# mLSTM and squared-ReLU FFN on one core: DRAM copies cut into 5 KB pieces and moved later, weights' fetches ahead of the loads of squares and of x's store

## The chip, the cores and the metric

The kernel runs on one core of a Trainium2 chip. The metric is the device time of an execution in microseconds (us); lower is better. The profile is one further execution with every instruction and DMA recorded; its span is 1 to 2 us below the device time.

## The reference, cut to what matters

```python
# 4 batches x 8 heads x 768 tokens x 40; k, q, v, gates, o_gate in float32
for t in range(S):                       # mLSTM: a recurrence per head
    C = f_stab * C + i_stab * outer(v_t, k_t);  n = f_stab * n + i_stab * k_t
    y_t = sigmoid(o_t) * (C @ q_t) / max(|n . q_t|, 1)
x = y.transpose(0, 2, 1, 3).reshape(3072, 320)
return (relu(x @ w_in) ** 2) @ w_out     # 320 -> 2048 -> 320; float64 weights
```

## The kernel before

The 3072 rows are 24 steps of 128 tokens. The mLSTM of a step gives x (128 x 320). The FFN works on groups of two steps: a first-layer product `ffn1` (reads x transposed, `xT`) and a second-layer product `ffn2` or `ffn2_fast` (makes the output y). Steps 0 to 5 form a start in which the weights are also brought in and rounded piece by piece (ScalarE, VectorE, GpSimd). From step 6 on, a loop runs four parts for each step `s` (`at` is 0 to 3): even steps carry an `ffn1`, odd steps a second layer. In this loop nothing is transposed on TensorE: k, q and x go through DRAM, come back as 32 x 32 squares side by side, and VectorE turns the squares.

```python
def pair_up(s):                          # a copy inside DRAM: heads in pairs
    b, c = divmod(s, NB)
    for n, src in enumerate((k, q)):
        nc.sync.dma_start(
            kq_d[s, n].rearrange("two j t d -> two j (t d)"),
            src[b, :, c * P : (c + 1) * P, :].rearrange("(j two) t d -> two j (t d)", two=2))

def squares_in(s, n, dst):               # four loads of squares from kq_d ... (cut)
def load(s):    ...                      # k, v; from step 7 on q's squares too (cut)
def load_kT(s): ...                      # k's squares (cut)

def store_rows(s):                       # x to DRAM, back as squares into xT
    t = st[s]["xT"] = xT_half(s).rearrange("p c t -> p (c t)")
    nc.sync.dma_start(x_d[s]..., st[s]["x"]...)
    for r in range(P // SQ):
        nc.sync.dma_start(t[r * SQ : (r + 1) * SQ]..., x_d[s, :, :, r * SQ : (r + 1) * SQ]...)

def turn_squares(s):
    nc.vector.transpose(st[s]["xT"], st[s]["xT"])

def ffn2_fast(g, step):                  # odd steps from 9 on; seven products, four parts
    ...
    elif step == 2:
        product(X5, S1, T[0]);  add(u22, u22, X5)
        product(Y6, ..., T[2]); add(m1, m1, Y6)
        nc.sync.dma_start(out[...], y1[:])       # y's store, on the same SP queue

def attend_on(s):
    do(attend, s); do(normalise, s)      # x is ready
    do(store_rows, s); do(load_kT, s + 2); do(load, s + 4); do(pair_up, s + 5)
    if 8 <= s < 20: load_o(s + 4)

for n, (which, g, i) in enumerate(parts):
    s, at = 6 + n // 4, n % 4
    if at == 0: do(score, s)
    if at == 1: attend_on(s)
    ...                                  # ffn1 of group g, or ffn2_fast(g, i)
    if at == 2: do(weigh_on, s + 1); do(turn_kq, s + 1)
    if at == 3: do(turn_squares, s)
    if n < 4:                            # the last weight pieces; each joined piece
        while rounding.done < NEXT[8 + n]:       # frees a buffer and fetches the next
            rounding.step()
```

The program keeps this order on each engine, and SP issues its DMAs in it: in the changed kernel x's store, whose data was ready at 476.6 us, goes out at 483.67, behind y's at 483.26 (shown below).

Of the kernel before, what the change touches and what calls it, by code (L numbers as in the profile page):

```python
# [9 lines left out]
F32 = mybir.dt.float32  # L10
# [7 lines left out]
P = 128  # L18
# [11 lines left out]
def kernel(  # L30
# [25 lines left out]
    nc = tc.nc  # L56
    B, H, S, D = q.shape
    BH = B * H
    NB = S // P
    NT = B * NB  # L60
    PR = H // 2
# [27 lines left out]

    A_d = nc.dram_tensor("a_rows", (BH, S), F32, kind="Internal").ap()  # L90

    kq_d = nc.dram_tensor("kq_rows", (NT, 2, 2, PR, P, D), F32, kind="Internal").ap()
    x_d = nc.dram_tensor("x_rows", (NT, 3, P, P), F32, kind="Internal").ap()


    NKQ = 4
# [168 lines left out]
    def load_parts(s):  # L265
        d = st.setdefault(s, {})
        kq, va = d["kq"], d["va"] = kq_b[s % NKQ], va_b[s % NKQ]
        return (kq[:, 0, :, :D], k), (kq[:, 1, :, :D], q), (va[:, :, :D], v)



    SQ = 32
    KQ_SQ, X_SQ = 7, 6

    def pair_up(s):
        b, c = divmod(s, NB)
        for n, src in enumerate((k, q)):
            nc.sync.dma_start(
                kq_d[s, n].rearrange("two j t d -> two j (t d)"),
                src[b, :, c * P : (c + 1) * P, :].rearrange("(j two) t d -> two j (t d)", two=2),  # L280
            )

    def squares_in(s, n, dst):

        for i in range(2):
            for e in range(0, D, SQ):
                w = min(SQ, D - e)
                nc.sync.dma_start(  # L288
                    dst[DP * i + e : DP * i + e + SQ].rearrange("p (b a) -> p b a", a=SQ)[:, :, :w],
                    kq_d[s, n, i, :, :, e : e + w].rearrange("j (m r) a -> r (j m) a", r=SQ),  # L290
                )

    def q_squares(s):
        return kq_b[s % NKQ][:, 1].rearrange("p h d -> p (h d)")

    def load(s):
        b, c = divmod(s, NB)
        (dk, sk), nat_q, vv = load_parts(s)
        for dst, src in ((dk, sk), nat_q, vv) if s < KQ_SQ else ((dk, sk), vv):
            nc.sync.dma_start(dst, src[b, :, c * P : (c + 1) * P, :].rearrange("h p d -> p h d"))  # L300
        if s >= KQ_SQ:
            if s < KQ_SQ + NKQ:
                nc.gpsimd.memset(q_squares(s), 0.0)
            squares_in(s, 1, q_squares(s))

    def load_kT(s):
        t = st[s]["kT"] = kT_b[s % NKT]
        squares_in(s, 0, t[:].rearrange("p j t -> p (j t)"))

    def turn_kq(s):  # L310
        d = st[s]
        nc.vector.transpose(d["kT"][:].rearrange("p j t -> p (j t)"), d["kT"][:].rearrange("p j t -> p (j t)"))
        d["qT"] = work.tile([P, PR, P], F32, name="qT")
        nc.vector.transpose(d["qT"][:].rearrange("p j t -> p (j t)"), q_squares(s))

    def load_o(s):
        b, c = divmod(s, NB)
        r, (s0, s1) = next((r, (a, z)) for r, (a, z) in enumerate(RUNS) if a <= s < z)
        if s == s0:
            st["og", r] = ld.tile([P, 4, H, D], F32, name="og")  # L320
        og = st.setdefault(s, {})["og"] = st["og", r][:, s - s0]
        nc.sync.dma_start(og, o_gate[b, :, c * P : (c + 1) * P, :].rearrange("h p d -> p h d"))
# [31 lines left out]
    def mask(s):  # L354

        A = st[s]["A"][0]
        nc.gpsimd.affine_select(  # L357
            A[:], A[:], compare_op=ALU.is_ge, fill=-1e30, base=0, pattern=[[0, H], [1, P]], channel_multiplier=-1,
        )
# [130 lines left out]
    def store_rows(s):  # L490
        t = st[s]["xT"] = xT_half(s).rearrange("p c t -> p (c t)")
        nc.sync.dma_start(x_d[s].rearrange("c t d -> t c d"), st[s]["x"][:].rearrange("p (c d) -> p c d", c=3))
        for r in range(P // SQ):
            nc.sync.dma_start(
                t[r * SQ : (r + 1) * SQ].rearrange("p (b a) -> p b a", a=SQ),
                x_d[s, :, :, r * SQ : (r + 1) * SQ].rearrange("c (n p) a -> p (c n) a", p=SQ),
# [44 lines left out]
    def ffn1(g, pp):  # L541
        ffn1_main(g, pp)
        ffn1_rest(g, pp, st["half"][0])

    def relu_half():
        if "half" in st:
            hs, g4 = st.pop("half")
            rs = []
            for h in hs:
                rs.append(ffn.tile([P, 2, WG], F32, name="r_sb", bufs=4))  # L550
                nc.scalar.activation(rs[-1][:], h[:], AF.Relu)  # L551
            st.setdefault("relu", []).append((rs, g4))
# [106 lines left out]
    def do(f, s):  # L659
        if 0 <= s < NT:  # L660
            f(s)
# [9 lines left out]
    def attend_on(s):  # L671
        do(attend, s)
        do(normalise, s)
        do(store_rows, s)
        do(load_kT, s + 2)
        do(load, s + 4)
        do(pair_up, s + 5)
        if 8 <= s < 20:
            load_o(s + 4)


    zeros = consts.tile([P, 16], BF16)
# [80 lines left out]
    for u in range(8):  # L763
        s = 2 + u // 2
        relu_half()
        if u % 2 == 0:
            if u == 0:
                ffn1(0, 0)
                scores(s)
                rounding.step()  # L770
            else:
                turn_rows(s - 1)
                scores(s)
                ffn1(u // 4, u % 4)
            if u == 2:
                rounding.words()
            weighted(s)
            if u == 2:
                mask(s + 1)
                rounding.join()  # L780
                rounding.join()
                weigh(s + 1, masked=True)
                rounding.words()
            else:
                weigh(s + 1)
                square_half()
        else:
            load_A(s + 2)
            for r in {3: (7, 8), 5: (9,), 7: (10,)}.get(u, ()):
                pair_up(r)  # L790
            for r in {1: (4,), 3: (5, 6), 5: (7,), 7: ()}[u]:
                load(r)
            if u == 5:
                for r in range(4, 8):
                    sigmoid(r)
            attend(s)
            if u == 3:
                square_half()
            rounding.join()
            normalise(s)  # L800
            for r in {5: (8,), 7: (9,)}.get(u, ()):
                load(r)
            if u > 4:
                load_o(2 * s)
                load_o(2 * s + 1)
            transposes(s + 1)
            rounding.words()
            ffn1(u // 4, u % 4)
            square_half()
        if u < 4:  # L810
            load_o(4 + u)
        while rounding.done < NEXT[u]:
            rounding.step()
    relu_half()
    square_half()
    turn_rows(5)
    load_A(8)
    load_kT(7)



# [7 lines left out]
    for n, (which, g, i) in enumerate(parts):  # L829
        s, at = 6 + n // 4, n % 4  # L830
        if n == 1:
            mask(s + 1)
        if n == 4:
            brought.close()
            late = ctx.enter_context(tc.tile_pool(name="late", bufs=1, side="right"))
        if at == 0:
            do(score, s)
        if at == 1:
            attend_on(s)
        if 5 <= n < 8:  # L840
            sums_of_weights(n - 5)
        if n == 9:
            sums_of_weights(3)
        if which == 1 and g > 2 and i in (0, 2):
            sums(g - 2, slice(2 * i, 2 * i + 4))
        if which == 2 and g >= NG - 3 and g + 1 < NG and i == 3:
            for one in (1, 2, 3):
                sums(g + 1, slice(0, NPAIR), (one,))
        if at == 3:
            if s % 4 == 3:  # L850
                for r in range(s + 1, min(s + 5, NT)):
                    sigmoid(r)
        if which == 1:
            ffn1_main(g, i)
            if i % 2 == 0:
                held = st["half"]
            else:

                both = held, st["half"]
                for more, half in enumerate(both):  # L860
                    ffn1_rest(g, i - 1 + more, half[0])
                for half in both:
                    st["half"] = half
                    relu_half()
                    square_half()
        elif g == 0:
            ffn2(g, *divmod(i, 2))
        else:
            ffn2_fast(g, i)
        if which == 2 and g >= NG - 3 and g + 1 < NG and i == 3:  # L870
            sums(g + 1, slice(0, NPAIR), (4,))
        if at == 2:
            do(weigh_on, s + 1)
            do(turn_kq, s + 1)
        if at == 3:
            do(turn_squares, s)
        if n < 4:
            while rounding.done < NEXT[8 + n]:
                rounding.step()


# [28 lines left out]
```

## Time and profile before

| | before |
|---|---|
| device time, median of 3 | 582.55 us (582.54 to 584.68) |
| profiled span | 582.1 us |
| TensorE busy | 547.4 us, 94% |
| largest idle time of TensorE | 18.56 us, 137.05 to 155.61 |
| TensorE idle from 177 to 532 us | 0.9 us |
| start of the first `ffn1` product that reads x from the loop | 177.71 us |

The last row is a mark. That product reads x of steps 6 and 7; what comes before it is the start with its data waits, what follows is the steady stage. So the time is 177.7 us of start and 404.4 us of the rest.

The profile's slices cut the span into 40 and give the busy share of each in tenths. A stretch line gives each engine's busy time in a chosen window, then the granted TensorE clock, the DMA share and GB/s. A timeline line gives start, duration, engine and line (SPq is SP's queue), output and input, and in brackets how long the engine had been idle and what the profile takes for the cause. Landings of DMAs, which these views do not show, were read from the semaphore updates in the trace. "Half clock" is a stretch in which the trace records half of TensorE's clock as granted; such records last 3.41 us or a multiple of it (3.41 to 27.31 us before), but for the one at the very end (1.30 us before). The steps of 3.41 us in which they begin and end are called windows below.

Of TensorE's small products, `tp` (reads qT and kT) makes the scores of a step, which VectorE turns into `P_sb`; `hp` multiplies `P_sb` with v; `dC` is the step's update of the state C. A "join" is the last step in rounding a weight piece. A "pair" is the copies of k and of q of one step.

### The profile page before, as it was taken

The page shows a single profiled execution, that of the slowest core. Times are in us where ns is not written, and L with a number is a line of the kernel's source. Part 1 is how long each engine was busy: PE and PEld are TensorE (multiplying, and loading weights), DVE is VectorE, ACT ScalarE, POOL GpSimd, SP SyncE. Part 2 cuts the span into 40 slices and gives each one's busy share as a digit, 9 for nine tenths or more (in the row PEclk, how much of TensorE's full clock was granted, in tenths as well). Part 3 has the DMA queues.
Part 4 walks back from the last instruction along what each step waited for, and adds up shares of the span by engine and source line. Part 5 has one row for each costly group of instructions (what it writes and reads, how often), then busy time and mean ns, then how long its engine had stood idle before and what let it go on. Part 6 is the DMA issues. An engine that isn't in the chain of part 4 may idle for free.

```text
span 582.1 us, 9738 instructions
## 1 busy us (share of the span) xinstructions
PE 547.4 (94%) x3688; PEld 487.2 (84%) x3689; DVE 329.2 (57%) x637; ACT 176.9 (30%) x448; POOL 99.6 (17%) x117
## 2 busy tenths in 40 slices
PE   9989888894399999999999999999999999999997
PEld 5878776683368898898998998998998998988996
DVE  7679965761455735746646556645555556434441
ACT  3777645331130510432313134113224304011000
POOL 3345433311211021110121212011111110000000
PEclk9988998897579999999999999999999999999999
DMA  9996486776043626644644654554573021100000
GB/s 195 233 213 138 130 183 114 197 166 125 14 69 99 114 57 139 116 80 120 116 73 119 119 84 123 109 95 110 120 130 74 15 48 28 25 26 2 24 24 23
DMA packets 221380, 58.06 MB, mean 100 GB/s; under 512 B 184357, under 2 KB 217893, under 8 KB 221061
## 3 DMA queue, kind: packets, MB, share of 16 engines
q1 hardware_dynamic: 221236, 57.24, 47.2%
q8 instruction: 29, 0.48, 0.4%
q10 hardware_dynamic: 96, 0.20, 0.1%
q14 instruction: 19, 0.15, 0.1%
HBM read 49.84 MB, written 13.14 MB: 108 GB/s over the span
## 4 chain that ended last, share of the span: by engine, by line
PE 80%; DVE 6%; DMA 5%; ACT 4%; SPq 2%; issue 1%; POOL 1%; DVEq 0%; ACTq 0%; POOLq 0%
PE h_ps L619 29%; PE h_ps L525 23%; PE hp L446 7%; PE h_ps L536 6%; DMA raw<-in_moe_w_out_dram 4%; PE tp L409 3%; PE dC L439 3%; PE h_ps L565 3%; PE hi L432 2%; SPq L288 1%; DVE g L558 1%; DVE mag L203 1%; PE idle L688 1%; ACT W_sb L372 1%; ACT mag L188 1%
## 5 line engine op out<-in xcount | busy, mean ns | idle before, releaser
L525 PE MATMUL h_ps<-xT,w_in 128*128 128x256 f32 x768 | 179.4, 390 | 5.8 <-ACT xT L510 2.7
L525 PEld LDWEIGHTS h_ps<-xT,w_in 128*128 128x128 f32 x768 | 145.7, 194 | 30.4 <-ACT xT L510 3.1
L558 DVE TENSOR_TENSOR g<-r_sb 128x512 f32<-128x512 f32 x96 | 64.1, 727 | 72.0 <-ACT r_sb L551 72.0
L551 ACT ACTIVATE r_sb<-h_ps 128x512 f32<-128x512 f32 x96 | 49.9, 600 | 160.5 <-PE h_ps L536 157.3
L619 PE MATMUL h_ps<-w_out,g 128*128 128x160 f32 x528 | 76.9, 302 | 0.0
L619 PEld LDWEIGHTS h_ps<-w_out,g 128*128 128x128 f32 x528 | 72.5, 190 | 1.3 <-ACT r_sb L551 0.3
L372 ACT ACTIVATE W_sb<-A_bc,b_T 128x128 f32<-128x128 f32 x176 | 53.9, 395 | 5.9 <-POOL A_bc L357 5.9
L619 PE MATMUL h_ps<-T,S 128*128 128x160 f32 x352 | 51.4, 299 | 0.0
L536 PE MATMUL h_ps<-xT,w_in 64*128 64x256 f32 x384 | 49.0, 391 | 0.0
L619 PEld LDWEIGHTS h_ps<-T,S 128*128 128x128 f32 x352 | 49.0, 190 | 0.0
L446 PE MATMUL hp<-va,P_sb 128*128 128x41 f32 x368 | 47.3, 292 | 0.0
L446 PEld LDWEIGHTS hp<-va,P_sb 128*128 128x128 f32 x368 | 46.3, 204 | 0.0
L536 PEld LDWEIGHTS h_ps<-xT,w_in 64*128 64x128 f32 x384 | 34.8, 186 | 12.5 <-issue 9.2
L383 POOL TENSOR_TENSOR vw<-va,W_sb 128x328 f32<-128x328 f32 x20 | 16.3, 813 | 160.0 <-ACT W_sb L372 134.2
L439 PE MATMUL dC<-vw,kq 128*128 128x82 f32 x160 | 22.2, 284 | 19.6 <-DVE P_sb L421 19.6
L633 DVE TENSOR_TENSOR y_sb<-y_sb,h_ps 128x160 f32<-128x160 f32 x33 | 10.6, 321 | 48.9 <-PE h_ps L619 48.9
L439 PEld LDWEIGHTS dC<-vw,kq 128*128 128x128 f32 x160 | 20.6, 199 | 20.2 <-issue 19.9
L465 POOL TENSOR_TENSOR C_sb<-C_sb,Cd 128x328 f32<-128x328 f32 x16 | 14.1, 880 | 125.6 <-DVE C_sb L457 125.2
L421 DVE TENSOR_TENSOR P_sb<-tp,W_sb 128x512 f32<-128x512 f32 x46 | 29.3, 678 | 10.3 <-PE tp L409 9.8
L633 DVE TENSOR_TENSOR y_sb<-h_ps,y_sb 128x160 f32<-128x160 f32 x22 | 7.1, 325 | 45.8 <-PE h_ps L619 29.1
L409 PE MATMUL tp<-qT,kT 40*128 40x128 f32 x384 | 26.9, 279 | 1.7 <-ACT qT L400 1.7
L409 PEld LDWEIGHTS tp<-qT,kT 40*128 40x128 f32 x384 | 24.2, 187 | 5.1 <-ACT qT L400 2.4
(100 smaller groups left out, 618.1 us busy)
## 6 DMA issues: line engine op xcount, KB each, us to landing
A_bc<-a_rows SPq DMA_DIRECT2D x22, 512.0 KB
raw<-in_moe_w_out_dram SPq DMA_DIRECT2D x16, 320.0 KB
raw<-in_moe_w_in_dram SPq DMA_DIRECT2D x8, 512.0 KB
kq<-in_k_dram SPq DMA_DIRECT2D x24, 160.0 KB
va<-in_v_dram SPq DMA_DIRECT2D x24, 160.0 KB
og<-in_o_gate_dram SPq DMA_DIRECT2D x24, 160.0 KB
out_dram<-y_sb SPq DMA_DIRECT2D x24, 160.0 KB
x_rows<-x_sb SPq DMA_DIRECT2D x18, 192.0 KB
```

Source lines behind the costliest of these rows:

```text
L372: nc.scalar.activation(d["W"][:, i * n + h, :], A[i][:, h, :], AF.Exp, bias=b_T[:, b, c, i * n + h : i * n + h + 1],)
L409: nc.tensor.matmul(sc[i][:, j, :], lhsT=d["kT"][rows, j, :], rhs=d["qT"][rows, j, :], start=True, stop=True,)
L421: nc.vector.tensor_tensor(t, d["sc"][i], d["W"][:].rearrange("p (j two) t -> p j two t", two=2)[:, :, i, :], op=ALU.mult,)
L439: nc.tensor.matmul(dC[:, j].rearrange("p h d -> p (h d)"), lhsT=d["kq"][:, 0, 2 * j : 2 * j + 2, :].rearrange("p h d -> p (h d)"), rhs=d[" ...
L446: nc.tensor.matmul(hp[:, h, :], lhsT=d["P"][h % 2][:, h // 2, :], rhs=d["va"][:, h, :], start=True, stop=True,)
L525: nc.tensor.matmul(hs[i][:, n, :], lhsT=w_in[:, a, fb * P : (fb + 1) * P], rhs=xT[:, :, a, :], start=(n == 0 and a == 0), stop=False,)
L536: nc.tensor.matmul(hs[i][:, n, :], lhsT=w_in2[rows, 2 * pp + n, :], rhs=xT[rows, :, 2, :], start=False, stop=(n == 1),)
L551: nc.scalar.activation(rs[-1][:], h[:], AF.Relu)
L558: nc.vector.tensor_tensor(g4[:, :, i, :], r[:], r[:], op=ALU.mult)
L565: nc.tensor.matmul(o_ps, lhsT=st["g2", g][:, fb, j * P : (j + 1) * P], rhs=w_out[:, fb, :], start=(fb == 0), stop=(fb == NF - 1),)
L619: nc.tensor.matmul(to, lhsT=lhsT[:, p], rhs=rhs[:, p, :], start=(start and p == 0), stop=(p == NPAIR - 1), skip_group_check=True,)
L633: add = lambda to, a, b: nc.vector.tensor_tensor(to, a, b, op=ALU.add)
```

## The change

The intent: the copies inside DRAM spread over more DMA engines and come later, so that they no longer hold up the start's loads; the last weight pieces go out ahead of everything that is needed later. In the loop SP's queue is put into a new order: the load, o and the copy at the end of the second part (`at == 1`), x's store and all squares at the end of the third.

```diff
+    SQ = 32
+    kq_d = nc.dram_tensor("kq_rows", (NT, 2, 2, PR, P // SQ, SQ * D + SQ), ...)   # padded
@@ pair_up: per tensor two copies, 4 x 4 pieces of 5 KB
-            nc.sync.dma_start(kq_d[s, n].rearrange("two j t d -> two j (t d)"), ...)
+            for i in range(2):
+                nc.sync.dma_start(kq_d[s, n, i, :, :, : SQ * D],
+                    src[b, i::2, c * P : (c + 1) * P, :].rearrange("j (m r) d -> j m (r d)", r=SQ))
@@ load_kT becomes load_squares: k's and q's squares together, no q squares in load
@@ attend_on
-        do(store_rows, s)
-        do(load_kT, s + 2)
-        do(load, s + 4)
-        do(pair_up, s + 5)
-        if 8 <= s < 20:
-            load_o(s + 4)
@@ the start: four calls of pair_up before the loads of step s become two, after them
-            for r in {3: (7, 8), 5: (9,), 7: (10,)}.get(u, ()):
-                pair_up(r)
+            for r in {5: (7,), 7: (8,)}.get(u, ()):
+                pair_up(r)
@@ the loop
         if at == 2:
+            do(store_rows, s)
+            do(load_squares, s + 2)
             do(weigh_on, s + 1)
...
         if n < 4:
             while rounding.done < NEXT[8 + n]:
                 rounding.step()
+        if at == 1:
+            do(load, s + 4)
+            if 8 <= s < 20:
+                load_o(s + 4)
+            do(pair_up, s + 3)
```

The built order of instructions on TensorE, VectorE and ScalarE is the same in both kernels. Only SP's queue and GpSimd's memsets differ.

More of the change, by code (lines that the diff above doesn't have):

```diff
@@ L90 @@
     A_d = nc.dram_tensor("a_rows", (BH, S), F32, kind="Internal").ap()
-    kq_d = nc.dram_tensor("kq_rows", (NT, 2, 2, PR, P, D), F32, kind="Internal").ap()
+    SQ = 32
+    kq_d = nc.dram_tensor("kq_rows", (NT, 2, 2, PR, P // SQ, SQ * D + SQ), F32, kind="Internal").ap()
     x_d = nc.dram_tensor("x_rows", (NT, 3, P, P), F32, kind="Internal").ap()
@@ L268, in load_parts @@
         return (kq[:, 0, :, :D], k), (kq[:, 1, :, :D], q), (va[:, :, :D], v)
-    SQ = 32
     KQ_SQ, X_SQ = 7, 6
@@ L277, in pair_up @@
         for n, src in enumerate((k, q)):
-            nc.sync.dma_start(
-                kq_d[s, n].rearrange("two j t d -> two j (t d)"),
-                src[b, :, c * P : (c + 1) * P, :].rearrange("(j two) t d -> two j (t d)", two=2),
-            )
+            for i in range(2):
+                nc.sync.dma_start(
+                    kq_d[s, n, i, :, :, : SQ * D],
+                    src[b, i::2, c * P : (c + 1) * P, :].rearrange("j (m r) d -> j m (r d)", r=SQ),
+                )
     def squares_in(s, n, dst):
@@ L289, in squares_in @@
                     dst[DP * i + e : DP * i + e + SQ].rearrange("p (b a) -> p b a", a=SQ)[:, :, :w],
-                    kq_d[s, n, i, :, :, e : e + w].rearrange("j (m r) a -> r (j m) a", r=SQ),
+                    kq_d[s, n, i, :, :, : SQ * D].rearrange("j m (r d) -> r (j m) d", d=D)[:, :, e : e + w],
                 )
@@ L300, in load, with load_squares @@
             nc.sync.dma_start(dst, src[b, :, c * P : (c + 1) * P, :].rearrange("h p d -> p h d"))
-        if s >= KQ_SQ:
-            if s < KQ_SQ + NKQ:
-                nc.gpsimd.memset(q_squares(s), 0.0)
-            squares_in(s, 1, q_squares(s))
-    def load_kT(s):
+    def load_squares(s):
+        if s < KQ_SQ + NKQ:
+            nc.gpsimd.memset(q_squares(s), 0.0)
         t = st[s]["kT"] = kT_b[s % NKT]
         squares_in(s, 0, t[:].rearrange("p j t -> p (j t)"))
+        squares_in(s, 1, q_squares(s))
     def turn_kq(s):
@@ L817 @@
     load_A(8)
-    load_kT(7)
+    load_squares(7)
     banks.close()
```

## The prediction

> **What bounds the kernel now.** I read the page's slices first, then stretches by engine, the waits, and the timelines of the DMA queue around the one big gap and around one later period. Slices (tenths busy, 14.55 us each; PEclk is the granted clock):
>
> ```profile
> PE   9989888894399999999999999999999999999997
> ...
> PEclk9988998897579999999999999999999999999999
> DMA  9996486776043626644644654554573021100000
> ```
>
> TensorE is full from slice 12 on; all that it lacks lies in the first 177 us, worst in slices 9 to 11, just where DMA falls to 0. The stretches (PE busy in the third column) put a number on it:
>
> ```profile
> 60.00:137.00 77.00, 68.84 (x425) 56.31 (x424) 52.05 (x103) 34.78 (x85) 25.05 (x30) 0.96 0.68 151
> 137.00:156.00 19.00, 0.44 (x3) 0.42 (x3) 5.16 (x11) 2.81 (x6) 1.00 (x2) 0.55 0.40 85
> 156.00:177.00 21.00, 21.00 (x78) 15.75 (x79) 9.11 (x16) 5.99 (x16) 3.91 (x5) 0.75 0.37 59
> 177.00:532.00 355.00, 354.10 (x2486) 324.75 (x2484) 198.45 (x397) 91.69 (x241) 43.63 (x48) 1.00 0.43 87
> ```
>
> So there are two stages: up to 156 us TensorE waits for data, after 177 us it is the bound, with 0.9 us idle in 355. A change can gain only in the first and can only lose in the second.
>
> The gap at 137: TensorE waits for VectorE's P_sb of step 7. VectorE stands behind a rounding step and behind ReLUs on ScalarE; ScalarE stands behind the last weight piece, issued last on SP's queue (the page's L278 is the copy inside DRAM). First fence: SP's timeline. Second: ScalarE's.
>
> ```profile
> 138.83 0.62 SPq L278 DMA_DIRECT2D kq_rows<-in_k_dram  x1
> 139.49 0.61 SPq L278 DMA_DIRECT2D kq_rows<-in_q_dram  x1
> 140.21 0.36 SPq L179 DMA_DIRECT2D raw<-in_moe_w_out_dram  x1
> ```
> ```profile
> 149.40 0.48 ACT L188 ACTIVATE mag<-raw 128x320 f32<-128x320 f32 x1 [16.06 <-DMA raw<-in_moe_w_out_dram]
> ```
>
> The piece's buffer was free when VectorE ended the join at 124.8 us, but it is issued at 140.2, after x's store, the squares, a load and a copy, and lands at 149.3 (landings I read from the semaphore updates in the trace). The two copies in front land at 145.4 and 148.5.
>
> [...] Before, the copy's source is 2x4x5120 and its destination 8x5120: 2 engines, 4 pieces of 20,480 bytes each. The trace agrees: such a piece takes 0.761 us (median of 272), four take 3.04, and queued copies land 3.05 us apart (68.36, 71.41, 74.45, 77.52). [...] loads issued at 64.5 and 64.9 behind four copies land at 78.2 and 78.9. [...] SP's loads of x's squares wait for x's store 18 times, 42.2 us in all. [...] the half-clock records last 3.413 us or multiples, [...] (idle 1.75 us at 84.6 and 2.12 at 99.4 each gave one such window; 18.6 us gave half clock to 166.4).
>
> **The change, part by part.** On TensorE, VectorE and ScalarE the built order of instructions is the same in both kernels; only POOL's memsets and SP's queue move.
>
> (a) Copies: each tensor's copy becomes two, of 4x4x1280 against 16x1280: 4 engines, 4 pieces of 5 KB. A pair of k and q took 2 x 3.05 = 6.1 us of the queue; now 4 x 4 x 0.19 = 3.05 (estimate: the same 27 GB/s). Ahead of x's first store, 3 pairs stand instead of 4 finished by then: 9 us instead of 24.
>
> (b) Early stage: TensorE's waits between 60 and 137 that end with a late DMA are 1.75 us (sigmoid's input at 84.9), 2.12 and 2.17 (weight pieces at 100.0 and 106.8), and the two half-clock windows cost 1.8 each (16 matmuls of L525 take 5.41 us instead of 3.65). That is 9.6 us; I take 6 as recovered, since VectorE and ScalarE remain in the way. The q squares of steps 8 and 9 leave this stage too.
>
> (c) The gap: the last piece can go at about 125 us instead of 140 and lands near 128. Next in VectorE's order is the transpose of x(6). SP: load(10), 0.9; pair 9, 2.5; x's store at 128.6; it lands behind the copies at about 134.6, as TensorE goes now; four loads of xT until 136.5, landed 138; transpose 0.6, last join 1.2, P_sb 0.6 to 1.2: 141. TensorE runs dry at 137.0: a gap of 4 instead of 18.6, so 14.5 saved. The slow clock behind it (hp 3.34 instead of 1.75, dC 1.97 instead of 0.95, L565 15.8 instead of 13.2: 5.1 us) falls to 1.6: 3.5 saved.
>
> Sum of gains: 6 + 14.5 + 3.5 = **24 us**.
>
> (d) x's store in the steady stage. This is where I expect the loss. The store of step s moves from its second part to the end of the third. In odd steps from 9 to 23 the third part is the second-layer product, and its own store of y (L651) now stands ahead on SP. Before, in the period of step 21 (SP; then VectorE; then TensorE):
>
> ```profile
> 462.94 0.38 SPq L492 DMA_DIRECT2D x_rows<-x_sb  x1
> 465.01 1.86 SPq L494 DMA_DIRECT2D xT<-x_rows  x4
> 466.97 2.01 SPq L288 DMA_DIRECT2D kT<-kq_rows  x4
> 469.56 0.36 SPq L651 DMA_DIRECT2D out_dram<-y_sb  x1
> ```
> ```profile
> 469.21 0.32 DVE L633 TENSOR_TENSOR y_sb<-y_sb,h_ps 128x160 f32<-128x160 f32 x1 [1.79 <-PE h_ps L619]
> ...
> 471.62 0.57 DVE L501 STREAM_TRANSPOSE xT<-xT 128x384 f32<-128x384 f32 x1
> ```
> ```profile
> 472.37 3.72 PE L525 MATMUL h_ps<-xT,w_in 128*128 128x256 f32 x16
> ```
>
> y is ready at 469.53, and the next first-layer product needs xT at 472.37: 2.84 us. The new chain from 469.53: y's issue 0.4, x's issue 0.4, landing 1.9 (1.68 with an empty queue, a little for y ahead of it), four issues 1.9, landing of the last 1.6, transpose 0.6, hand-over 0.1: 6.9 us. TensorE stands 6.9 - 2.84 = **4.1 us**, in each of 8 odd steps (9, 11, ... 23; I read the margin in steps 21 and 23, 2.84 and 2.71, and the order is the same in all): 33 us. [...] a half-clock window follows, 1.6 us on the mean over its phase: 13 us. Step 7 has an ordinary product, but y's store of its second part, load(11) and pair 10 stand ahead of x's store: about 3 us. In even steps the transpose comes some 14 us after x is ready (453.68 against 439.3), and even with 2.5 us for copies and 3 for the load the rows land near 449: nothing lost.
>
> Sum of losses: 33 + 13 + 3 = **49 us**. Net: 582.5 - 24 + 49 = 607; I say 605, leaning a little to a smaller clock cost.
>
> **The rivals.** *Gain without loss*: were x's store not held by y's, the time would be 582.5 - 24 = 558. For it: the early gap is large and certain, and the change is plainly aimed at it. Against it: SP issues in order, and the built order shows y's store directly ahead of x's in every odd step from 9. *Same wait, other cause*: the early gap stays because x(6)'s rows, now issued behind the weights, take the place of the weight piece; then the gap is 8 to 10 us and the time about 612. For it: x's store, the copy and the loads stand in one queue. Against it: 15 us of two-engine copies have left that queue. *Stalls without the clock*: 594. For it: two idle times of about 2 us (66.3 and 107.8) brought no half clock. [...] *More engines per copy* [...]: 2 to 3 us less in (c) and step 7, not decisive.
>
> **Range and chances.** Gains between 18 and 32, losses between 36 and 54: 592 to 617. Within 2% means 570.9 to 594.2, reached if the stalls are 3 us or the clock costs nothing and the early gain is full: 0.15. Faster would need the stalls to be absent: 0.05.
>
> **What would show it right or wrong.** In the profile after: the idle time before P_sb's consumer (dC) at some 4 us instead of 18.6 shows (c); copies landing 0.76 us apart show (a); L525 waiting for the transpose of xT, 8 or 9 times at 4 us, and half-clock windows after each, show (d). If TensorE is still busy for 354 of 355 us in the steady stage, (d) is wrong, and with it the sign. If the waits are there but the clock stays whole, only the 13 us fall. If the first stage gains under 15 us, VectorE or ScalarE bounds it and not the DMA.

Cut from the recorded text, where marked: rules for copies, queues and the clock that no trace of this case shows. The measured numbers beside them stand. No term of the sum was cut: gains of 6 + 14.5 + 3.5 = 24 us, losses of 33 + 13 + 3 = 49, and 582.5 - 24 + 49 = 607. That a wait of 4.1 us must bring half clock was not shown. The 1.6 us for each of eight waits, and the 1.6 left in (c), are estimates; the trace before has two waits of about 2 us, each with a half-clock window behind it that cost about 1.8 us (after the first, 16 matmuls in 5.41 us instead of 3.65). The 2 to 3 us of the last rival is an estimate too. That a copy runs on two engines before, and on four after, is seen in the DMA records: of the time in which pieces of 20,480 bytes are in flight (124 us), two are in flight for 115.7; in the changed kernel the pieces of 5 KB take 0.196 us (median of 1088), mostly four at once (48.6 of 78 us).

## The result

The changed kernel is slower: 609.71 us (median of 4, 608.73 to 611.17) against 582.92 us (median of 4). The ratio is 1.0455, 95% interval 1.0424 to 1.0487. A ratio is the mean time of one kernel's fast runs over that of the other's of the same rounds, so it is not quite the ratio of these medians.

The slices of the changed kernel's page:

```profile
PE   9989899979799799799799799799899979969997
...
PEclk9989999979899899799799999989989989979999
DMA  9985988542652553444445354454344031010000
```

The start no longer has its hole, but from the ninth slice on TensorE falls to 7 tenths in about every third slice, and the clock falls with it. The stretches, same columns as before:

```profile
60.00:137.00 77.00, 71.64 (x449) 60.20 (x449) 58.99 (x120) 37.18 (x90) 27.85 (x33) 0.94 0.75 159
137.00:156.00 19.00, 14.93 (x65) 10.57 (x64) 7.39 (x10) 6.13 (x16) 1.44 (x2) 0.95 0.38 74
177.00:532.00 355.00, 328.35 (x2261) 300.76 (x2258) 175.16 (x356) 82.40 (x220) 39.65 (x44) 0.95 0.40 82
```

In the first two stretches TensorE is busy for 17.3 us more than before; in the last for 25.8 us less, at a clock of 0.95 instead of 1.00. The gap before dC of step 7, in TensorE's timeline before and after:

```profile
155.61 1.97 PE L439 MATMUL dC<-vw,kq 128*128 128x82 f32 x8 [18.56 <-DVE P_sb L421]
```
```profile
129.58 1.98 PE L440 MATMUL dC<-vw,kq 128*128 128x82 f32 x8 [3.61 <-issue]
```

The period of step 21 in the changed kernel, SP's timeline, then VectorE's, then TensorE's:

```profile
483.26 0.36 SPq L652 DMA_DIRECT2D out_dram<-y_sb  x1
483.67 0.43 SPq L493 DMA_DIRECT2D x_rows<-x_sb  x1
485.84 1.86 SPq L495 DMA_DIRECT2D xT<-x_rows  x4
```
```profile
482.91 0.32 DVE L634 TENSOR_TENSOR y_sb<-y_sb,h_ps 128x160 f32<-128x160 f32 x1 [1.79 <-PE h_ps L620]
...
489.32 0.58 DVE L502 STREAM_TRANSPOSE xT<-xT 128x384 f32<-128x384 f32 x1 [3.92 <-DMA xT<-x_rows]
```
```profile
489.95 5.41 PE L526 MATMUL h_ps<-xT,w_in 128*128 128x256 f32 x16 [3.82 <-DVE xT L502]
```

x itself had been ready since 476.6 us (end of L483's copy), but its store goes out at 483.67, straight behind y's store, which waits for y at 483.23. The rows are back at 489.2, the transpose ends at 489.9, and TensorE has stood for 3.82 us. Its next 16 matmuls then take 5.41 us instead of 3.72 (472.37 before): half clock.

With the mark of the first `ffn1` product the account is:

| | before | changed | difference |
|---|---|---|---|
| start, up to that product (us) | 177.71 | 154.96 | -22.75 |
| of it: TensorE idle just before dC of step 7 | 18.56 | 3.61 | -14.95 |
| of it: TensorE idle just before the product (step 7) | 0 | 4.08 | +4.08 |
| the rest, product to end | 404.4 | 452.0 | +47.6 |
| of it: 8 waits of odd steps | 0.90 | 31.66 | +30.8 |
| of it: what is left, taken as slow clock | | | +16.8 |

The last row agrees with the clock's records: in the nine half-clock records after 150 us (without the one at the very end) TensorE is busy for 34.4 us; half of that, 17.2 us, is an estimate of the loss.

Of TensorE's nine long waits at the first layer (step 7's and the eight), the profile puts six down to another cause. This is the list of TensorE's waits of the changed kernel (total, times, longest):

```profile
PE h_ps L526 <- DMA kT<-kq_rows: 22.7, 6, 4.1
PE h_ps L526 <- DVE xT L502: 13.0, 3, 5.0
```

Line 526 does not read kT. A squares' load happened to land near the end of the wait, and the view names the last event on the semaphores concerned. The first experiment tests whether it is more than that.

### The profile page after: what moved, and what is told of

The parts are those of the page before. It is cut to its first block, busy times and chain, and to the rows that moved or that the text cites. A ratio compares the mean times of both kernels' runs of the same rounds, so it can differ in the third digit from the quotient of the medians.

```text
span 607.0 us, 9781 instructions
## 1 busy us (share of the span) xinstructions
PE 559.6 (92%) x3689; PEld 496.1 (82%) x3689; DVE 328.6 (54%) x637; ACT 176.3 (29%) x448; POOL 99.3 (16%) x117
## 4 chain that ended last, share of the span: by engine, by line
PE 81%; DMA 7%; DVE 4%; SPq 4%; issue 2%; ACT 2%; POOL 0%; DVEq 0%; POOLq 0%
PE h_ps L526 29%; PE h_ps L620 25%; PE hp L447 7%; PE h_ps L537 7%; DMA x_rows<-x_sb 4%; PE dC L440 3%; PE hi L433 3%; SPq L495 2%; PE tp L410 2%; DMA kT<-kq_rows 2%; PE h_ps L566 2%; PE idle L683 1%; DMA xT<-x_rows 1%; PE A_ps L349 1%; ACT W_sb L373 1%
## 5 line engine op out<-in xcount | busy, mean ns | idle before, releaser
L526 PE MATMUL h_ps<-xT,w_in 128*128 128x256 f32 x768 | 192.8, 411 | 36.3 <-DMA kT<-kq_rows 22.7
L526 PEld LDWEIGHTS h_ps<-xT,w_in 128*128 128x128 f32 x768 | 155.5, 207 | 65.3 <-DVE xT L502 33.2
L559 DVE TENSOR_TENSOR g<-r_sb 128x512 f32<-128x512 f32 x96 | 62.4, 708 | 57.6 <-ACT r_sb L552 57.6
L502 DVE STREAM_TRANSPOSE xT<-xT 128x384 f32<-128x384 f32 x18 | 10.4, 575 | 46.5 <-DMA xT<-x_rows 46.5
```

Source lines behind the costliest of these rows:

```text
L526: nc.tensor.matmul(hs[i][:, n, :], lhsT=w_in[:, a, fb * P : (fb + 1) * P], rhs=xT[:, :, a, :], start=(n == 0 and a == 0), stop=False,)
L559: nc.vector.tensor_tensor(g4[:, :, i, :], r[:], r[:], op=ALU.mult)
```

## The experiments

Theory A: in odd steps from 9 on, y's store stands ahead of x's on SP, which issues in order (y's at 483.26, then x's at 483.67, in SP's timeline of step 21 above); x's rows come back 4 us too late, and each such wait also costs a stretch of half clock. Theory B, for the start: a copy on two engines closes the queue for 3.05 us, and the last weight piece stood behind squares and such a copy. Rivals are named with each run. Each run had 3 timed rounds against the kernel before on the same chip (4 runs of the kernel, 7 or 8 of before). All results were correct.

### a_xfirst: x's store ahead of y's, in odd steps alone

```diff
 # changed kernel
+        if at == 2 and which == 2 and g > 0:
+            do(store_rows, s)            # ahead of ffn2_fast, so ahead of y's store
         ...
         if at == 2:
-            do(store_rows, s)
+            if not (which == 2 and g > 0):
+                do(store_rows, s)
```

> The changed kernel, but in odd steps from 9 on x's store and its loads of squares stand ahead of the product whose result y is stored, so y's store no longer holds them. Theory (SP issues in order, y's store holds x's): the 8 waits of TensorE of 3.6 to 5.0 us (31.7 us) and some 16 us of half clock go, 609.7 becomes 560 to 566. Rival (the loads and copies inside DRAM ahead of x's store, or the loads of squares behind it, hold the rows of x): those stand where they stood, so the waits stay and the time is 603 to 610.

Measured: 569.38 us, ratio 0.9767 (0.9739 to 0.9795). Theory A stands: moving x's store, with its loads of squares, ahead of y's gives back 40 us. The squares' loads that the wait list had named still follow in the same place, so they were not the cause. The forecast (560 to 566) was 3 us too good. In seven of the eight places a wait of 0.68 to 1.37 us is left, 6.4 us in all and without a half clock (the last of them, 0.90 us, is there before the change too). SP's timeline and TensorE in the worst of them:

```profile
360.41 1.27 SPq L280 DMA_DIRECT2D kq_rows<-in_q_dram  x2
361.77 0.39 SPq L493 DMA_DIRECT2D x_rows<-x_sb  x1
366.31 2.73 SPq L495 DMA_DIRECT2D xT<-x_rows  x4
369.13 0.41 SPq L652 DMA_DIRECT2D out_dram<-y_sb  x1
```
```profile
371.38 3.72 PE L526 MATMUL h_ps<-xT,w_in 128*128 128x256 f32 x16 [1.37 <-DVE xT L502]
```

x's store now goes out 7 us ahead of y's, but stands behind the load and the copies, and takes 4.5 us until the rows can be asked for, where 2.2 us were enough above. So the rival was not wholly wrong: the load and the copies ahead of x's store cost about 0.9 us in each of six steps; step 21, which has neither, has no wait. This run does not part the two.

### a_xpart1: x's store ahead of the load and the copies, in every step

```diff
 # changed kernel
         if at == 2:
-            do(store_rows, s)
             do(load_squares, s + 2)
 ...
         if at == 1:
+            do(store_rows, s)
             do(load, s + 4)
```

> The changed kernel, but x's store stands right behind the weights' fetches at the end of the second part, ahead of the load and the copies, in every step. Theory: besides the 8 waits, the waits of step 7 (4.1 us) and before dC of step 7 (3.6 us) go with their half clock (about 4 us): 548 to 556, better than both kernels. Rival (weights or VectorE set the early end anyway): the two early waits stay and the time is that of the kernel with only the odd steps mended, 560 to 566.

Measured: 549.12 us, ratio 0.9408 (0.9385 to 0.9430): the best version, faster than both kernels. All waits of step 7 and before dC are gone, with the 0.7 to 1.4 us that the copies had left. Its page:

```profile
PE 537.7 (98%) x3688; PEld 479.9 (88%) x3689; DVE 328.6 (60%) x637; ACT 176.7 (32%) x448; POOL 101.6 (19%) x117
...
PE   9989899999999999999999999999999999999997
...
PEclk9998989999999999999999999999999999999999
```

With x's store put ahead, then, the rest of the change together is worth some 34 us against the kernel before. What each part is worth, the b_ runs show in part.

### a_warm: dummy matmuls in the waits

```diff
 # changed kernel
         if at == 0:
             do(score, s)
+            if which == 1 and g > 2:
+                idle(16)                 # 16 matmuls of zeros, 512 columns
```

> The changed kernel with 16 dummy matmuls of 512 columns (about 3.4 us) put into each of the 8 waits (and step 7's), nothing else moved; the product after the wait needs the same data at the same time. Theory (the half clock after a wait costs real time): the waits stay as time, but the half-clock windows go, 609.7 becomes 592 to 597. Rival (half clock after so short a wait costs little, the rest of the loss is elsewhere): 606 to 613.

Measured: 592.69 us against 609.71 of the changed kernel (ratio to before 1.0167, 1.0139 to 1.0195). The chain of x's rows is untouched and the real product still waits for it, yet 17 us are gone. The dummies stand in step 7's wait too. One wait in TensorE's timeline (the dummies begin at 473.92, ahead of the window shown, and end 3.45 us later; 15 of 16 are recorded):

```profile
474.80 2.57 PE L683 MATMUL idle<-zeros 128*128 128x512 bf16 x11
477.57 3.72 PE L526 MATMUL h_ps<-xT,w_in 128*128 128x256 f32 x16 [0.20 <-DVE xT L502]
```

The 16 matmuls after it take 3.72 us, not 5.41. No half-clock record is left after 140 us but the one at the very end. So the loss of 47.6 us is about two thirds waiting and one third clock, as the account had it.

### b_xlate: the late store alone, on the kernel before

```diff
 # kernel before
-        do(store_rows, s)
+        if s < 8:
+            do(store_rows, s)
 ...
         if at == 2:
+            if s >= 8:
+                do(store_rows, s)
             do(weigh_on, s + 1)
```

> The kernel before, with one part of the change alone: from step 8 on x's store moves behind the third part, so behind y's store in odd steps; copies, squares and loads stay where they were. Theory: the early stage is that of before, the loss of 47 us comes in full, 582.9 becomes 625 to 634. Rival (it takes the moved loads of squares and copies too): under 595.

Measured: 644.01 us, ratio 1.1041 (1.0986 to 1.1096). The loss comes with this part alone, so the direction holds, but it is 10 us above the range expected. The waits of steps 19, 21 and 23 are 3.84, 4.10 and 5.00 us (3.82, 3.82 and 5.01 in the changed kernel); those of steps 9 to 17 are 5.25 to 7.07 us. SP's timeline at step 9, where the old copies are still issued, and at step 21, which has none:

```profile
210.01 0.63 SPq L278 DMA_DIRECT2D kq_rows<-in_k_dram  x1
210.69 0.60 SPq L278 DMA_DIRECT2D kq_rows<-in_q_dram  x1
...
216.38 0.36 SPq L651 DMA_DIRECT2D out_dram<-y_sb  x1
216.79 0.43 SPq L492 DMA_DIRECT2D x_rows<-x_sb  x1
221.50 1.85 SPq L494 DMA_DIRECT2D xT<-x_rows  x4
```
```profile
516.45 0.43 SPq L492 DMA_DIRECT2D x_rows<-x_sb  x1
518.61 1.85 SPq L494 DMA_DIRECT2D xT<-x_rows  x4
```

At step 9 the copies land at 216.8 and 219.8 us; x's rows can be asked for 4.7 us after the store is issued, at step 21 after 2.2 us. I had left this out of the forecast. The next run tests it.

### b_xlate4: the late store with the new copies, on the kernel before

The edit is that of b_xlate together with that of b_small below.

> The kernel before with two parts: 4-engine copies of 5 KB, and from step 8 on x's store behind y's. With the big copies the late store had cost 61 us instead of 47, its waits 5.2 to 7.1 us in steps 9 to 17 and 3.8 to 5.0 in the last three, which have no copy ahead. Theory (two big copies ahead of x's store on the same engines delay its landing): the waits of steps 9 to 17 fall to 3.6 to 4.5 us, the time is that with small copies alone (568) plus 45 to 50: 613 to 618. Rival (the loads and squares ahead of it, which stay, make the surplus): over 622.

Measured: 615.05 us, ratio 1.0543 (1.0510 to 1.0576). The waits of steps 9 to 17 are now 3.62 to 4.13 us, and x's rows at step 9 can be asked for 2.2 us after the store's issue. The surplus was the old copies. The late store costs 47 us on top of b_small's 568. In this run no squares follow x's store, and the view of waits names what really ends the wait:

```profile
PE h_ps L527 <- DVE xT L503: 32.4, 8, 5.1
```

### b_four and b_small: the copies alone, on the kernel before

```diff
 # b_four: four engines, pieces still 20 KB, no padding
-            nc.sync.dma_start(
-                kq_d[s, n].rearrange("two j t d -> two j (t d)"),
-                src[b, :, ...].rearrange("(j two) t d -> two j (t d)", two=2))
+            for i in range(2):
+                nc.sync.dma_start(
+                    kq_d[s, n, i].rearrange("j t d -> j (t d)"),
+                    src[b, i::2, ...].rearrange("j t d -> j (t d)"))
 # b_small: pair_up, the padded kq_d and squares_in as in the change; nothing else
```

> The kernel before, each copy inside DRAM split in two by pair, pieces still 20 KB, at the same places: [...] 4 engines. Theory (the number of engines sets how long a copy closes the queue, piece size doesn't matter): a pair takes 3 us of the queue instead of 6.1; two pairs that close the loads at 60 to 77 us and pair 11 ahead of the last weight piece each give back 3 us, so the time falls by 4 to 10 us, 573 to 579. Rival (the size of the pieces is what counts): 582 to 584.

> The kernel before with part one of the change alone: pieces of 5 KB in rows padded by 128 B, 4 engines, at the same places. Theory: the same as with 4 engines and 20 KB pieces, within 1 per cent (573 to 579). Rival (small pieces let other transfers through between them): at least 6 us faster than that.

(b_four's run shows four as the distance of the landings below, 0.76 us, the time of one 20 KB piece.)

Measured: b_four 567.88 us, ratio 0.9746 (0.9719 to 0.9774); b_small 568.03 us, ratio 0.9745 (0.9720 to 0.9770). The two are equal, so the size of the pieces does not matter here, and neither does the padding. What both share is four engines instead of two, and with it twice as many copies of half the size; these two go together and were not parted. The copies of b_four land about 0.76 us apart (65.12, 65.87, 66.63 us ...), a fourth of before's 3.05, and there are twice as many of them. My forecast of the size was too small: 15 us, not 4 to 10. The gap before dC fell by 5.1 us (18.56 to 13.43), with less half clock behind it, and the waits of 1.75 and 2.17 us, with both early half-clock windows, are gone. In TensorE's waits of b_four:

```profile
PE dC L440 <- issue: 13.4, 1, 13.4
```

### a_big: the changed kernel with the old copies

The edit puts back `pair_up`, `kq_d` and `squares_in` of the kernel before; places and order stay those of the change.

> The changed kernel with the old copies (2 engines, 20 KB pieces) at the new places. Theory: once they are late, a copy's size costs only where x's store stands right behind it and TensorE waits for it: 3 us before dC of step 7 and 3 us at step 7's product, nothing at the odd steps where y's store ends the wait: 609.7 becomes 613 to 620. Rival (the pieces make the early gain): the early stage falls back by 10 us or more, over 620.

Measured: 615.62 us, ratio 1.0575 (1.0531 to 1.0619). Against the changed kernel's 609.71 that is 6 us, as expected: the wait before dC is 8.13 us instead of 3.61, that of step 7 is 7.30 instead of 4.08, and the eight odd steps are 3.8 to 4.9. (The profiled execution was the slowest of the four, 619.66.) Once the copies are late, running them on two engines is nearly harmless, but only nearly: it shows again where x's store stands right behind them (the first two waits).

### b_weights: the last weight piece ahead, on the kernel before

```diff
 # kernel before; in attend_on only store_rows stays
-        do(load_kT, s + 2)
-        do(load, s + 4)
-        do(pair_up, s + 5)
-        if 8 <= s < 20: load_o(s + 4)
 ... # and at the end of the pass, behind the weights' steps:
+        if at == 1:
+            do(load_kT, s + 2); do(load, s + 4); do(pair_up, s + 5)
+            if 8 <= s < 20: load_o(s + 4)
```

> The kernel before with one part alone: at the end of the second part the loads of squares, the load and the copy stand behind the fetch of the last weight piece; x's store stays ahead of it, copies stay big and early. Theory (the 18.6 us gap is the last piece's place in the queue): it is issued near 133 us instead of 140 and not behind a copy, the gap falls to 3 to 8 us with its half clock, 582.9 becomes 566 to 572. Rival (the squares or VectorE end the gap anyway): 580 or more.

Measured: 570.68 us, ratio 0.9792 (0.9772 to 0.9812; the verdict at 2% is "unclear" since the interval spans it, but the medians are 12.4 us apart, and the slowest of its runs, 570.77, lies 10.4 us under the fastest of before, 581.21). The piece goes out at 133.96 us and the gap is 5.75 us; SP's timeline, and the line of TensorE's waits (a second wait of 1.1 us is in its total):

```profile
133.96 0.40 SPq L179 DMA_DIRECT2D raw<-in_moe_w_out_dram  x1
```
```profile
PE dC L439 <- DVE P_sb L421: 6.8, 2, 5.8
```

The waits at 84 and 99 us stay, at 1.72 and 3.22 us (1.75 and 2.12 before), as they should, for nothing was changed there.

### b_both: new copies and the weights' order, x's store in its old place

The edit is that of b_small together with that of b_weights.

> The kernel before with 4-engine copies of 5 KB and the last weight fetch ahead of the squares; x's store stays ahead of both. Theory (two separate causes of the early waits, 15.1 and 12.4 us alone): they add up, 553 to 558. Rival (both mend the same wait before dC): 564 to 568.

Measured: 557.85 us, ratio 0.9546 (0.9502 to 0.9590). The two parts add up: 583.7 less 15.1 and 12.4 would be 556.2. It stays 8.7 us behind a_xpart1. Its wait before dC is still 2.17 us, with half clock for 10.2 us, and 1.5 us are left at 98 us, with one half-clock record (100.54 to 103.96). a_xpart1 has none of these. It differs in x's store, now behind the weight pieces, and in having fewer copies and no q squares in the start; which of these counts was not separated.

## Why the prediction was right

**What bounds it.** Right: two stages, and the change gained in the first and lost in the second.

**(a) Copies.** Right in mechanism, and b_four with b_small shows it alone (567.88 and 568.03 us): four engines with twice as many copies, not smaller pieces.

**(b) Early waits.** I took 6 of 9.6 us. All three waits and both half-clock windows went, so the term should have been 9.6. VectorE and ScalarE did not stand in the way.

**(c) The gap.** A wait of 4 was forecast and 3.61 measured, by the path forecast: the piece no longer ends it, x(6)'s rows do. VectorE waits 3.60 us for them until 127.21, turns them, joins and makes P_sb. (The forecast's times are on the axis of the kernel before; TensorE in fact ran dry at 125.97, 11 us earlier: (b)'s 9.6, and 1.4 that lie before 60 us, where both kernels have the same order: hp of step 3 begins at 59.76 and at 58.35.) The term for the clock behind the gap failed: I wrote that 5.1 us would fall to 1.6. The record of half clock behind the short gap still lasts 10.24 us, and from dC to the scores behind the 48 second-layer matmuls 20.15 us pass instead of 21.01: 0.9 us was saved instead of 3.5. The errors of (b) and (c) are opposite and partly cancelled. The start up to step 7's wait gained 26.8 us (177.71 less 150.89) where 24 were forecast: 9.6 + 14.95 + 0.9 + 1.4.

**(d) x's store.** Right, and the steps of the chain too: 6.9 us from y to the turned xT forecast; 483.23 to 489.90, 6.7 us, measured. The waits came to 3.6 to 5.0 us each, against 4.1. Step 23 stands out because its margin was misread as 2.71: before the change TensorE already waits 0.90 us there, so y is only 1.8 us ahead of the moment it runs dry (511.24 and 513.06), and 5.01 less 0.90 is the 4.1 again. The clock was put at 13 us for eight waits and came to 16.8 for nine: step 7's wait brought a half-clock record too, and of the nine records four last two windows (6.83 us) and five one (3.41); a_warm shows it as real time. Step 7: 4.1 us against about 3.

**Luck.** Gains of 26.8 us and losses of 51.7 (30.8, 16.8 and step 7's 4.1) were each 3 us above the forecast, 24 and 49. So the net of 25 us came out in the profiles (24.9) although its parts did not, and the lean from 607 to 605, toward a smaller clock cost, went the wrong way.

**Small misreadings.** TensorE's gap lies in slices 10 and 11, not 9 to 11. The join that frees the piece's buffer begins at 124.76 and ends at 125.25 us; the sum in (c) does not hang on it. The forecast took a share of idle time in a window as the mark for a half clock; the traces show no such mark: see the last section.

**The rivals.** *Gain without loss* (558) is near b_both, x's store in its old place, at 557.9; with x's store merely taken ahead of y's (a_xfirst) it is 569.4, with it ahead of the load and the copies too (a_xpart1) 549.1. *Stalls without the clock* (594) is close to what a_warm gives (592.7), but only with dummy matmuls. *Same wait, other cause* was refuted: the gap before dC is 3.6 us; what is left of it is x(6)'s rows. *More engines per copy* was not the case: in the changed kernel the first copies land 0.8 us apart (85.96, 86.74, 87.53, 88.31), the forecast's 0.76 of four engines within little, and four pieces are in flight at once.

Why half clock lasts one window after some of the nine waits and two after others, can be read from the changed kernel's trace: it goes with where the wait lies in the windows (no run moves it on its own). In the four long cases the half-clock record begins 2.2 to 2.8 us before the wait ends (247.84 against 250.13, for instance), so most of its first window is still idle; in the five short ones it begins at the wait's end or after it (490.19 against 489.95). What stays open: why half clock held through whole windows of work behind dC, and what idle time in a window brings half clock.

## What to carry to other kernels

SP issued its queue in order here, and x's store waited for the data of y's ahead of it (x was ready at 476.6 us, its store went out at 483.67): put the store whose data has long been ready, and whose readers are close, in front of the one that still waits for the bound engine. Look at how many engines a DRAM copy runs on: here copies on two engines landed 3.05 us apart and held up the loads behind them, and four engines, with twice as many copies of half the size, gave back 15 us (b_four). A wait of 4 us on TensorE cost about 6 here (35.7 us in nine waits, 16.8 of clock), since a half-clock record followed each; count both.

## What the traces show of the clock and of DMA

- Half clock. Idle times of 1.75 and 2.12 us (before, up to 86.39 and 101.51), each inside one window, were each followed by a half-clock window of 3.41 us. How much idle time it takes is not shown: a window with 1.09 us idle among short matmuls (before, 36.69 to 40.10) and one with 1.49 us (changed kernel, 244.43 to 247.84) were followed by half clock, one with 1.62 us idle was not (before, 108.37 to 111.78). And after 18.56 us idle TensorE resumed at 155.61 us with half clock until 166.39; after only 3.61 us (changed kernel) it resumed at 129.58 with half clock until 138.61. That is 10.8 and 9.0 us of work without a pause, with two whole busy windows (156.15 to 162.98) and one (131.79 to 135.20) before the last half-clock window; both began with short matmuls of 82 and 41 columns.
- What copies on two engines cost the transfers behind them: four such copies of 160 KB, issued from 60.95 to 63.76 (before), landed 3.05 us apart, the last at 77.52; two loads issued at 64.5 and 64.9 landed at 78.2 and 78.9; and the second of these issues took SP 8.90 us.
- A store to DRAM and a load of the same rows back, issued from SP with nothing ahead of it on the queue: a store of 192 KB could be read 2.07 us after its issue began, and the last of the four loads landed 3.47 us after that (before, 462.94, 465.01 and 468.48).
